# Two matrix layers behind a chunked attention: the second layer in two passes, each by Strassen's seven block products

## Chip, cores and metric

One core of one Trainium2 chip. The metric is the device time of one execution in microseconds (us); lower is better.

## What is computed

```python
def _moe_ref(x, w_in, w_out, alpha):          # first layer, 4608 tokens, 512 -> 2048 -> 512
    h = x @ w_in
    g = np.maximum(h, 0.0) + alpha * np.minimum(h, 0.0)
    return (g @ w_out).astype(np.float32)

def _moe2_ref(x, w_in, w_out):                # second layer, the same sizes
    h = x @ w_in
    g = np.where(h > 0.0, h, np.exp(np.minimum(h, 0.0)) - 1.0)
    return (g @ w_out).astype(np.float32)

def reference(...):
    attn_out = _attn_ref(q, k, v)             # softmax attention within chunks of 64 tokens, 8 batches x 8 heads
    x = attn_out.transpose(0, 2, 1, 3).reshape(B * S, H * D)
    return _moe2_ref(_moe_ref(x, ...), ...)
```

All weights come as float64 and are turned into float32 on the chip.

## The kernel before

Every large product is made of three matmuls: each operand is split into a high part that TensorE takes as it is (type fp32r) and a low part, the rest, and high x high, high x low and low x high are added up in PSUM. A split is one ScalarE copy (high) and one VectorE subtraction (low).

The 4608 tokens are nine blocks of 512 (`TB`), the 2048 inner features sixteen groups of 128 (`f`). One step of a block is `first(ph, j, f)` (L430: 4 input chunks x 3 matmuls of 128x512 into a bank `h`), the activation and split of its result (`after_first`), and `second(ph, j, f)` (L502: 4 output chunks x 3 matmuls into the four banks `acc`, which add up over the sixteen `f`). `ph` is the layer. Each matmul has its own load of a 128x128 operand.

The program is in three parts. `start()` puts out the beginning by a table of costs and due times (attention of the first tokens, the first layer's `first` of three blocks, the weights of layer one). `catch_up()` does the `second` of those blocks. `rest()` goes over the steps of both layers in a fixed order: at step s it issues `first` of step s + 2, one stage of the attention of the next block (`att_step`: scores, transposed weights by way of `turn` on VectorE and a pass through memory that `bring` fetches into `pbd`, product with v), and `second` of step s. `flush()` puts what engines other than TensorE do for a stage one stage later in the order. DMAs are all issued by SyncE's queue (SP), in order.

The second layer's weights are made during the first: at every second step `tick()` takes one 128x512 piece from float64 to float32 (two ScalarE operations, L150 and L175; three on VectorE, L157, L161 and L168; one on GpSimd, L180), and stores it (256 KB); `w_back` reloads the 32 pieces at the end of layer one and splits them into the tiles of layer one's weights, as these come free. The first layer's result goes to memory (`mid`), 512 tokens at a time, and is reloaded for the second layer. Both layers of a step stay on the chip: g is never stored in layer two.

Of the kernel before, what the change touches and what calls it, by code (L numbers as in the profile page):

```python
# [17 lines left out]
P = 128  # L18
CH = 64
SQ = 32  # L20
TB = 512

# [41 lines left out]
def tile_chunk_attention_prelu_elu(  # L64
# [27 lines left out]
    const = ctx.enter_context(tc.tile_pool(name="const", bufs=1))  # L92
    wp = ctx.enter_context(tc.tile_pool(name="wp", bufs=1))
    xp = ctx.enter_context(tc.tile_pool(name="xp", bufs=1))
    gp = ctx.enter_context(tc.tile_pool(name="gp", bufs=3))
    w64p = ctx.enter_context(tc.tile_pool(name="w64p", bufs=3))
    ldp = ctx.enter_context(tc.tile_pool(name="ldp", bufs=3))
    ap_ = ctx.enter_context(tc.tile_pool(name="ap", bufs=2))
    st_p = ctx.enter_context(tc.tile_pool(name="st", bufs=2))
    dram = ctx.enter_context(tc.tile_pool(name="dram", bufs=1, space=bass.MemoryType.DRAM))  # L100
    ps_acc = ctx.enter_context(tc.tile_pool(name="ps_acc", bufs=1, space=bass.MemoryType.PSUM))
    ps_h = ctx.enter_context(tc.tile_pool(name="ps_h", bufs=2, space=bass.MemoryType.PSUM))
    ps_a = ctx.enter_context(tc.tile_pool(name="ps_a", bufs=2, space=bass.MemoryType.PSUM))

    def w_tile(name, f, dtype=F32R):
# [6 lines left out]
    kbd = [const.tile([P, 2, NHP * 2, CH], F32, name="kbd0")]  # L112
    kbd += [w_tile("out", f, F32).rearrange("p c (h k) -> p c h k", k=CH) for f in (6, 7, 8)]
    pbd = const.tile([P, 2, NHP * 2, CH], F32, name="pbd")
    mid = [dram.tile([P, KDM, TB], F32, name=f"mid{j}") for j in range(NB)]
# [18 lines left out]
    pieces = [(1, "in", f, w1_in) for f in range(KFF)] + [(1, "out", f, w1_out) for f in range(KFF)]  # L134
    for f in range(KFF):
        pieces += [(2, "in", f, w2_in), (2, "out", f, w2_out)]
    raw, single = [], []

    def w_load():
        ph, name, f, w = pieces.pop(0)  # L140
        w64 = w64p.tile([P, KDM, P], I64, tag="w64", name="w64")
        nc.sync.dma_start(out=w64, in_=w_src(w, name, f))
        raw.append((ph, name, f, w64.rearrange("p k f -> p (k f)")))

    def w_abs():
# [20 lines left out]
    def w_join():  # L166
        words, t = single[-1][3:5]
        nc.vector.scalar_tensor_tensor(  # L168
            out=t, in0=words[:, 1], scalar=-0x40000000, in1=t, op0=ALU.bitwise_and, op1=ALU.bitwise_or
        )  # L170

    def w_low():

        words, low = single[-1][3], single[-1][5]
        nc.scalar.activation(out=words[:, 0], in_=low, func=AF.Copy, scale=2.0**-13)  # L175

    def w_add():

        words, t = single[-1][3:5]
        nc.gpsimd.tensor_tensor(out=t, in0=t, in1=words[:, 0], op=ALU.add)  # L180
# [8 lines left out]

    def tick():  # L190


        if single:
            ph, name, f, t = (single[0][i] for i in (0, 1, 2, 4))
            single.pop(0)
            nc.sync.dma_start(out=w_mid[name, f], in_=t.bitcast(F32))
        if len(raw) > 1 or raw and not pieces:
            w_abs()
            w_low()
            w_clamp()  # L200
            w_join()
            w_add()
        while pieces and len(raw) < 2:
            w_load()


    back, landed = [], []

    def w_back(most=3):
        while landed:  # L210
            name, f, t = landed.pop(0)
            wt[f"2{name}", f] = hl = w_hi(name, f, t)
# [13 lines left out]
    def load_qk(t):  # L226

        i = place(t)
        for c in range(2):
            nc.sync.dma_start(  # L230
                out=kbd[i][c * CH:(c + 1) * CH, c].rearrange("p h k -> p (h k)"),
                in_=kT[t, c * CH:(c + 1) * CH, :],
            )
        if i:
            qv = w_tile("out", 8 + i, F32)
            q_t[t], v_t[t] = qv[:, 0], qv[:, 1]
        else:
            q_t[t] = ldp.tile([P, NHP * 2 * CH], F32, tag="q", name="q", bufs=1)
        nc.sync.dma_start(out=q_t[t], in_=qT[t])

    def load_v(t):
        if not place(t):
            v_t[t] = ldp.tile([P, NHP * 2 * CH], F32, tag="v", name="v", bufs=1)
# [96 lines left out]
    def put_x(t, x):  # L340
        j, i = divmod(t, TPB)
        if i == 0:
            xf_t[1, j] = xp.tile([P, KDM, TB], F32, tag="xf", name="xf")
# [117 lines left out]
    def after_first(ph, j, f, h):  # L461
        if ph == 1:
            gf = prelu(f, h)
        else:
            gf = gp.tile([P, TB], F32, tag="gf", name="gf", bufs=2)

            nc.vector.tensor_scalar_min(gf, h, 0.0)  # L467
            nc.scalar.activation(out=gf, in_=gf, func=AF.Exp)  # L468
            nc.vector.scalar_tensor_tensor(  # L469
                out=gf, in0=gf, scalar=-1.0, in1=h, op0=ALU.add, op1=ALU.max  # L470
            )
# [16 lines left out]
    def second(ph, j, f):  # L488
# [6 lines left out]
        for e in range(KDM):  # L495
            a = slice(e * P, (e + 1) * P)
            if ph == 1:
                pairs = ((whi[:, a], ghi), (whi[:, a], glo), (wlo[:, a], ghi))
            else:
                pairs = ((ghi[:, a], whi), (ghi[:, a], wlo), (glo[:, a], whi))  # L500
# [6 lines left out]
        w_back(0)  # L507
        for e in range(KDM):
            if (ph, j) < (1, AHEAD) and e < 2:
                st = gp.tile([P, TB], F32, tag="gf", name="ost", bufs=2)  # L510
            elif (ph, j) < (1, AHEAD) or (ph, j) == (2, NB - 1) and e < 2:
                st = ldp.tile([P, TB], F32, tag="wt", name="ost", bufs=2)
            else:
                st = ldp.tile([P, TB], F32, tag="ld", name="ost")
            if (ph, j, e) == (2, NB - 1, KDM - 1):

                r0 = j * TB + e * P
                half = slice(0, TB // 2), slice(TB // 2, TB)
                nc.scalar.copy(st[:, half[0]], acc[e][:, half[0]])
                nc.vector.tensor_copy(st[:, half[1]], acc[e][:, half[1]])  # L520
                for queue, a in zip((nc.scalar, nc.sync), half):
                    queue.dma_start(out=out[r0:r0 + P, a], in_=st[:, a])
                return
# [4 lines left out]
            if ph == 1:  # L528
                nc.sync.dma_start(out=mid[j][:, e, :], in_=st)
            else:  # L530
                r0 = j * TB + e * P
                nc.sync.dma_start(out=out[r0:r0 + P, :], in_=st)

    def start():
# [38 lines left out]
        for i in range(2 * KFF):  # L573
# [168 lines left out]

    def rest():
        steps = [(ph, j, f) for ph in (1, 2) for j in range(AHEAD if ph == 1 else 0, NB) for f in range(KFF)]
        nxt = 2
        stages = []
        for s, (ph, j, f) in enumerate(steps):
# [14 lines left out]
            if (ph, j) == (1, NB - 1):  # L762
                back.append(("out", f))
            if ph == 1 and s % 2 == 0:
                tick()

            if (ph, j) != (1, NB - 1) or f not in range(KFF - 4, KFF - 1):
                w_back()
            b = 0 if (ph, j) == (1, NB - 1) else j + 1 if ph == 2 else NB
            if b < NB and f == 2:  # L770
                xf_t[2, b] = xp.tile([P, KDM, TB], F32, tag="xf", name="xf")
                nc.sync.dma_start(out=xf_t[2, b], in_=mid[b])

# [51 lines left out]
```

## Time and profile before

| | |
|---|---|
| median of 3 runs | 1679.34 us (1678.82 to 1680.45) |
| the profiled execution, span | 1679.1 us |
| TensorE matmuls (PE) | busy 1667.7 us, 99%, 8163 records |
| weight loads (PEld) | 1373.0 us, 82% |
| VectorE, ScalarE, GpSimd | 52%, 31%, 10% |
| DMA | 146 MB, mean 87 GB/s |

The busy time of an engine adds up the records of its instructions; a matmul's record lasts from its start to its modelled end and overlaps the next one's, and the loads of weights overlap the matmuls. The span runs from the first to the last instruction. PEclk is the granted clock of TensorE as a share of 2.4 GHz.

### The profile page before, as it was taken

What the parts mean: (1) busy time and instruction counts of PE and PEld (TensorE: products, weight loads), DVE (VectorE), ACT (ScalarE), POOL (GpSimd) and SP (SyncE); (2) the same over time, 40 slices, a digit from 0 to 9 for tenths busy, and PEclk for the clock granted to TensorE, in tenths of its full rate; (3) what the DMA queues carried; (4) which work ended last, traced back from release to release, by engine and by line L of the source; (5) the groups of instructions that cost most, each with busy time, mean ns of one, the idle gap of its engine ahead of it and who ended that gap; (6) DMA issues with size and microseconds to landing.
All of it is one profiled execution on the core that took longest, in us unless ns stands there. A gap on an engine that the chain in (4) does not pass through costs nothing.

```text
span 1679.1 us, 20843 instructions
## 1 busy us (share of the span) xinstructions
PE 1667.7 (99%) x8163; PEld 1373.0 (82%) x8163; DVE 868.2 (52%) x1374; ACT 522.9 (31%) x890; POOL 167.3 (10%) x144
## 2 busy tenths in 40 slices
PE   9999999999999999999999999999999999999999
PEld 7788887888888888888888888888888888888887
DVE  7868753456657566654444343434343434343443
ACT  5866422222223232311323232223222323222222
POOL 2322200011111111100242000000000000000000
PEclk9999999999999999999999999999999999999999
DMA  7756545344435443331332010101010101010000
GB/s 233 246 174 198 191 153 163 117 126 128 136 113 157 135 130 114 118 101 32 119 95 88 1 50 1 51 0 51 0 51 0 51 1 51 0 41 10 19 7 25
DMA packets 90002, 146.08 MB, mean 87 GB/s; under 512 B 9264, under 2 KB 38192, under 8 KB 88752
## 3 DMA queue, kind: packets, MB, share of 16 engines
q1 hardware_dynamic: 89760, 144.62, 27.1%
q8 instruction: 64, 1.05, 0.3%
q14 instruction: 34, 0.28, 0.1%
q10 hardware_dynamic: 144, 0.13, 0.0%
HBM read 98.57 MB, written 46.14 MB: 86 GB/s over the span
## 4 chain that ended last, share of the span: by engine, by line
PE 97%; ACT 1%; DVE 1%; DMA 1%; issue 0%; SPq 0%; POOL 0%; ACTq 0%; POOLq 0%; DVEq 0%
PE acc L502 46%; PE h L430 46%; PE x L332 2%; PE s L252 2%; PE unread L549 1%; ACT pbd L297 0%; DMA pbd<-p 0%; PE pt L291 0%; DMA p<-tp 0%; SPq L311 0%; ACT neg L445 0%; DVE mx L263 0%; DVE p L265 0%; DVE sm L274 0%; DVE sm L275 0%
## 5 line engine op out<-in xcount | busy, mean ns | idle before, releaser
L430 PE MATMUL h<-xhi,in 128*128 128x512 f32 x2176 | 713.6, 390 | 0.0
L430 PEld LDWEIGHTS h<-xhi,in 128*128 128x128 f32 x2176 | 408.6, 188 | 85.6 <-issue 0.9
L430 PE MATMUL h<-xlo,in 128*128 128x512 f32 x1088 | 424.1, 390 | 0.1
L502 PE MATMUL acc<-ghi,out 128*128 128x512 f32 x1152 | 375.6, 392 | 0.0
L502 PE MATMUL acc<-out,ghi 128*128 128x512 f32 x1152 | 354.9, 389 | 0.0
L477 ACT ACTIVATE ghi<-gf 128x512 fp32r<-128x512 f32 x240 | 151.6, 632 | 501.2 <-DVE gf L458 376.1
L482 DVE TENSOR_TENSOR glo<-gf,ghi 128x512 fp32r<-128x512 f32 x240 | 166.8, 695 | 182.7 <-ACT ghi L477 182.7
L502 PEld LDWEIGHTS acc<-ghi,out 128*128 128x128 f32 x1152 | 216.3, 188 | 48.6 <-issue 3.3
L502 PEld LDWEIGHTS acc<-out,ghi 128*128 128x128 f32 x1152 | 216.3, 188 | 44.8
L430 PEld LDWEIGHTS h<-xlo,in 128*128 128x128 f32 x1088 | 204.4, 188 | 43.0 <-DVE xlo L410 0.7
L468 ACT ACTIVATE gf<-gf 128x512 f32<-128x512 f32 x144 | 91.0, 632 | 448.5 <-DVE gf L467 448.5
L502 PE MATMUL acc<-glo,out 128*128 128x512 f32 x576 | 224.6, 390 | 0.0
L502 PE MATMUL acc<-out,glo 128*128 128x512 f32 x576 | 224.4, 390 | 0.0
L467 DVE TENSOR_SCALAR gf<-h 128x512 f32<-128x512 f32 x144 | 99.4, 690 | 220.3 <-PE h L430 220.3
L469 DVE SCALAR_TENSOR_TENSOR gf<-gf,h 128x512 f32<-128x512 f32 x144 | 99.1, 688 | 111.5 <-ACT gf L468 111.5
L455 DVE TENSOR_SCALAR gf<-h,alpha_sb 128x512 f32<-128x512 f32 x112 | 84.0, 750 | 138.7 <-PE h L430 138.2
L502 PEld LDWEIGHTS acc<-out,glo 128*128 128x128 f32 x576 | 108.2, 188 | 22.4
L502 PEld LDWEIGHTS acc<-glo,out 128*128 128x128 f32 x576 | 108.2, 188 | 21.5
L180 POOL TENSOR_TENSOR wt<-wt,w 128x512 int32<-128x512 int32 x64 | 84.7, 1323 | 386.6 <-DVE wt L168 203.3
L458 DVE SCALAR_TENSOR_TENSOR gf<-h,gf 128x512 f32<-128x512 f32 x112 | 77.4, 691 | 3.8
L280 POOL TENSOR_TENSOR p<-p,sm 128x512 f32<-128x512 f32 x32 | 36.2, 1130 | 264.8 <-DVE sm L276 259.2
L482 DVE TENSOR_TENSOR glo<-gl,ghi 128x512 fp32r<-128x512 f32 x48 | 32.8, 687 | 42.1 <-ACT ghi L477 42.1
(66 smaller groups left out, 950.1 us busy)
## 6 DMA issues: line engine op xcount, KB each, us to landing
w<-moe_w_in SPq DMA_DIRECT2D x32, 512.0 KB, 4.5
w<-moe_w_out SPq DMA_DIRECT2D x32, 512.0 KB, 4.1
gl<-g SPq DMA_DIRECT2D x48, 256.0 KB, 2.9
mid<-ost SPq DMA_DIRECT2D x36, 256.0 KB, 2.5
xf<-mid SPq DMA_DIRECT2D x9, 1024.0 KB, 5.2
out<-ost SPq DMA_DIRECT2D x35, 256.0 KB, 2.0
g<-pos SPq DMA_DIRECT2D x32, 256.0 KB, 2.8
kbd<-k_t SPq DMA_DIRECT2D x54, 128.0 KB, 2.8
```

The source lines that it names most:

```text
L180: nc.gpsimd.tensor_tensor(out=t, in0=t, in1=words[:, 0], op=ALU.add)
L252: nc.tensor.matmul(s[par * CH:(par + 1) * CH, hp], qq[:, h * CH:(h + 1) * CH], kbd[place(t)][:, :, h, :], start=True, stop=True,)
L280: (nc.vector if t < TPB else nc.gpsimd).tensor_tensor(out=p_t[t], in0=p_t[t], in1=sm, op=ALU.mult)
L430: nc.tensor.matmul(h, w[:, a], x, start=(kk == 0 and m == 0), stop=(kk == KDM - 1 and m == 2),)
L455: nc.vector.tensor_scalar(out=gf, in0=h, scalar1=0.0, scalar2=alpha_sb[:, f:f + 1], op0=ALU.min, op1=ALU.mult)
L458: nc.vector.scalar_tensor_tensor(out=gf, in0=h, scalar=0.0, in1=gf, op0=ALU.max, op1=ALU.add)
L467: nc.vector.tensor_scalar_min(gf, h, 0.0)
L468: nc.scalar.activation(out=gf, in_=gf, func=AF.Exp)
L469: nc.vector.scalar_tensor_tensor(out=gf, in0=gf, scalar=-1.0, in1=h, op0=ALU.add, op1=ALU.max)
L477: nc.scalar.activation(out=ghi, in_=gf, func=AF.Copy)
L482: nc.vector.tensor_sub(glo, gf, ghi.bitcast(F32))
L502: nc.tensor.matmul(acc[e], l, r, start=(f == 0 and m == 0), stop=(f == KFF - 1 and m == 2))
```

## The change

The first layer keeps its products. The second is done in two passes over all tokens: first all of x @ w_in with the activation, whose result g goes to memory (`gm`), then all of g @ w_out. Each pass takes 768 tokens at a time (six pairs of halves of 384, `HT`) and halves the summed dimension and the output dimension too, so that a product of 2x2 by 2x2 blocks comes from seven block products rather than eight (Strassen's scheme, in Winograd's form: four sums on either side, and sums of products, some of which PSUM does by adding a product onto an earlier one). In the first pass a step is one product of one quarter of 256 columns of each half: 12 matmuls of 128x384 (L945); in the second it is one product and one quarter of the summed dimension: 18 matmuls of 128x256 (L1044), with g as the loaded operand. Either has 28 steps for a token pair.

The seven combinations of the blocks of w_in and of w_out are made and split during the first layer, by the generator `convert` (80 pieces, of which `rest` takes one at each step but the last of a block), and stored split, 56 tiles of 512 KB (`w_mid`). They are brought back into the tiles of the weights that are done with (`bring_w2`). The sums of x and of g, their splits, the temporaries and the activation are done a step or more ahead or behind on VectorE and ScalarE. At the change of layer pools of tiles are closed and opened anew, the eight banks of PSUM with them: a0, a1, d and b of two banks each.

```diff
-    def tick():
...
-    def w_back(most=3):
...
+    def convert(cw, cb):
...
+            def split(k, src):
+                r = cb.tile([P, 2, KDM * P], F32R, tag="R", name="R")
+                nc.scalar.activation(out=shape(r[:, 0]), in_=src, func=AF.Copy)
+                nc.vector.tensor_sub(shape(r[:, 1]), src, shape(r[:, 0]).bitcast(F32))
+                m = u * NPROD + k if name == "in" else k * 4 + u
+                nc.sync.dma_start(out=w_mid[name, m], in_=r.bitcast(F32))
+
+            for t in (p0[:, 0], p0[:, 1], p1[:, 0]):
+                piece(t)
+                yield
+            piece(p1[:, 1])
+            split(0, a11)
+            yield
+            split(3, a12)
+            nc.vector.tensor_tensor(out=sm, in0=a21, in1=a22, op=ALU.add)
+            yield
...
     def rest():
-        steps = [(ph, j, f) for ph in (1, 2) for j in range(AHEAD if ph == 1 else 0, NB) for f in range(KFF)]
+        steps = [(1, j, f) for j in range(AHEAD, NB) for f in range(KFF)]
...
+        cw = open_pool("cw", conv, bufs=2, reuse_waits="tile")
+        cb = open_pool("cb", conv, bufs=1, reuse_waits="tile")
...
-            if ph == 1 and s % 2 == 0:
-                tick()
...
+            if f < KFF - 1:
+                next(ticks, None)
+            if j == NB - 1:
+                bring_w2("in", f)
+                if f >= 4:
+                    bring_w2("in", KFF + f - 4)
...
+                if 8 <= f < 13:
+                    prod(f - 8)
...
+    SUMS = {1: (X, Y, X), 2: (X, W, X), 4: (Y, W, Y), 5: (Z, Z, X)}
+    SRC = (X, X, X, Z, Y, W, Z)
...
+    def banks_for(k, a):
...
+        return bank["adabada"[k]]
...
+    def combine(k, acc, shape):
+        if k < 3:
+            temp[k] = slot(TEMP[k], f"t{k}", shape=shape)
+            nc.scalar.copy(temp[k], acc)
+        elif k < 6:
+            t = temp[k - 3]
+            nc.vector.tensor_tensor(out=t, in0=t, in1=acc, op=ALU.add)
+            return t
+        else:
+            return acc
...
+    def elu_exp(c):
...
+        nc.scalar.activation(out=r, in_=c, func=AF.Relu, scale=-1.0)
+        nc.scalar.activation(out=r, in_=r, func=AF.Exp, scale=-1.0)
+        return r
+
+    def elu_join(p, sw, k, c, r):
+        nc.vector.scalar_tensor_tensor(out=r, in0=r, scalar=-1.0, in1=c, op0=ALU.add, op1=ALU.max)
+        fh, th = QUARTER[k]
+        nc.sync.dma_start(out=gm[4 * fh + sw, 2 * p + th], in_=r)
+
+    def layer2_first():
...
+            for i in range(2):
+                for kk in range(2):
+                    a = slice((2 * i + kk) * P, (2 * i + kk + 1) * P)
+                    for m, (h, x) in enumerate(((0, xh), (0, xl), (1, xh))):
+                        nc.tensor.matmul(
+                            acc[:, i, :HT], w[:, h, a], x[:, kk, :],
...
+            c = combine(k, acc[:, :, :HT], (P, 2, HT))
...
+            if last:
+                if r >= 2:
+                    bring_w2("out", r - 2)
+                if 8 <= r < 12:
+                    g_bring(0, X, r - 8)
...
+    def layer2_second():
...
+            for i, t in order:
+                a = slice(t * P, (t + 1) * P)
+                whi, wlo = w[:, 0, i * HD:(i + 1) * HD], w[:, 1, i * HD:(i + 1) * HD]
+                for m, (l, x) in enumerate(((gh, whi), (gh, wlo), (gl, whi))):
+                    nc.tensor.matmul(
+                        acc[:, t * HD:(t + 1) * HD], l[:, i, a], x,
...
+            if prev:
+                finish(*prev)
+            prev = (p, k, acc) if q == 3 else None
+            g_sum(n + 3)
+            g_split(n + 2)
```

How the order of the instructions moves, at three places. The first is TensorE at the change of layer, in the changed kernel: the last four output chunks of layer one (L477), then the first step of the first pass (a is a pair of banks, w2in a split tile of combined weights).

```order
L477 MATMUL acc_7358<-ghi,out_2446 128x512
L477 MATMUL acc_7358<-glo,out_2446 128x512
L477 MATMUL acc_7358<-ghi,out_2446 128x512
L945 MATMUL a_7959<-xhi_7700,w2in_7383 128x384 [waits DMAHW5_49,DVE_49,Activation_49]
L945 MATMUL a_7959<-xlo_7701,w2in_7383 128x384
L945 MATMUL a_7959<-xhi_7700,w2in_7383 128x384 x2
L945 MATMUL a_7959<-xlo_7701,w2in_7383 128x384
```

The first product stands right behind the last matmul of layer one and waits for VectorE and ScalarE, which empty acc; before, the matmuls into `h` of the next block stood there.

The second is TensorE at the change of pass: the last matmuls of the first pass, then the second (w2out: combined weights, ghi and glo the loaded operand).

```order
L945 MATMUL a_10884<-xlo_10549,w2in_8046 128x384
L945 MATMUL a_10884<-xhi_10548,w2in_8046 128x384
L1044 MATMUL a_11040<-w2out_10531,ghi_10952 128x256 [waits DMAHW3_49,PE_49,Activation_49]
L1044 MATMUL a_11040<-w2out_10531,ghi_10952 128x256
L1044 MATMUL a_11040<-w2out_10531,glo_10953 128x256
```

The stream goes on into the other pair of banks, and waits for a weight tile and a split of g.

The third is VectorE in layer one, around the turn of the attention's weights (`STREAM_TRANSPOSE`). Before:

```order
L482 TENSOR_TENSOR glo<-gf,ghi 128x512 [waits Activation_49]
L157 TENSOR_SCALAR wt<-wt 128x512 [waits DMAHW4_49,Activation_49]
L161 TENSOR_SCALAR wt<-wt 128x512 [waits DVE_49]
L168 SCALAR_TENSOR_TENSOR wt<-w_3924,wt 128x512 [waits DMAHW2_49,DVE_49]
L455 TENSOR_SCALAR gf<-h,alpha_sb 128x512 [waits PE_49]
L458 SCALAR_TENSOR_TENSOR gf<-h,gf 128x512 [waits DVE_49]
L482 TENSOR_TENSOR glo<-gf,ghi 128x512 [waits Activation_49]
L303 STREAM_TRANSPOSE tp<-p 128x4x4x32 [waits DMAHW3_49,Pool_49]
L455 TENSOR_SCALAR gf<-h,alpha_sb 128x512 [waits PE_49]
```

In the changed kernel (P: a piece, S: a sum, R: the buffer of a split):

```order
L290 STREAM_TRANSPOSE tp<-p 128x4x4x32 [waits DMAHW6_49,Pool_49]
L161 TENSOR_SCALAR P_4990<-P_4990 128x512 [waits Activation_49]
L165 TENSOR_SCALAR P_4990<-P_4990 128x512 [waits DVE_49]
L171 SCALAR_TENSOR_TENSOR P_4990<-w_5114,P_4990 128x512 [waits DMAHW5_49,DVE_49]
L754 TENSOR_TENSOR R<-P_4989,R 128x512 [waits DMAHW0_49,Activation_49]
L442 TENSOR_SCALAR gf<-h,alpha_sb 128x512 [waits PE_49]
L445 SCALAR_TENSOR_TENSOR gf<-h,gf 128x512 [waits DVE_49]
L460 TENSOR_TENSOR glo<-gf,ghi 128x512 [waits Activation_49]
L754 TENSOR_TENSOR R<-P_4989,R 128x512 [waits DMAHW0_49,Activation_49]
L765 TENSOR_TENSOR S<-P_4990 128x512 [waits Pool_49]
L442 TENSOR_SCALAR gf<-h,alpha_sb 128x512 [waits PE_49]
```

Work on the weights stands behind every step's glo now, not every second one's, and a split waits for ScalarE and for a DMA.

## Rows read from the trace of the kernel before

**Rows 1.** The page: busy time by engine, and the chain that ended last, by engine.
```profile
PE 1667.7 (99%) x8163; PEld 1373.0 (82%) x8163; DVE 868.2 (52%) x1374; ACT 522.9 (31%) x890; POOL 167.3 (10%) x144
...
PE 97%; ACT 1%; DVE 1%; DMA 1%; issue 0%; SPq 0%; POOL 0%; ACTq 0%; POOLq 0%; DVEq 0%
```

**Rows 2.** Stretches: length, busy PE, PEld, DVE, ACT, POOL, granted clock, DMA share, GB/s.
```profile
0.00:35.00 35.00, 32.34 (x244) 24.37 (x245) 23.09 (x47) 17.13 (x28) 9.13 (x19) 1.00 0.77 237
340.00:860.00 520.00, 519.61 (x2733) 427.70 (x2732) 311.01 (x504) 138.26 (x239) 83.50 (x68) 1.00 0.38 116
892.00:1675.00 783.00, 783.00 (x3456) 648.65 (x3454) 328.89 (x483) 212.58 (x348) 10.23 (x8) 1.00 0.07 26
```

**Rows 3.** Costliest groups, layer two's matmuls and loads: operands, count | busy, mean ns.
```profile
L502 PE MATMUL acc<-out,ghi 128*128 128x512 f32 x1152 | 354.9, 389 | 0.0
...
L502 PEld LDWEIGHTS acc<-out,ghi 128*128 128x128 f32 x1152 | 216.3, 188 | 44.8
```

**Rows 4.** The chain in order of time, layers one and two: start, us, what.
```profile
165.05 2.72 PE acc L502 x12
...
1487.62 2.72 PE acc L502 x12
```

**Rows 5.** Timeline of PE, the first ten and the first nine matmuls: start, us, what.
```profile
1.45 4.63 PE L549 MATMUL unread<-zeros 128*128 128x512 f32 x10 [1.45 <-DVE zeros L544]
...
1.45 4.21 PE L549 MATMUL unread<-zeros 128*128 128x512 f32 x9 [1.45 <-DVE zeros L544]
```

**Rows 6.** Timeline of the weight loads, 29.5 to 31.2 us, after a pause.
```profile
30.13 0.19 PEld L430 LDWEIGHTS h<-xlo,in 128*128 128x128 f32 x1 [0.43 <-DVE xlo L615]
30.24 0.42 PEld L430 LDWEIGHTS h<-xhi,in 128*128 128x128 f32 x2
30.71 0.19 PEld L430 LDWEIGHTS h<-xlo,in 128*128 128x128 f32 x1
30.95 0.42 PEld L430 LDWEIGHTS h<-xhi,in 128*128 128x128 f32 x2
```

**Rows 7.** Timeline of the weight loads, 30 to 34 us: a stage of the attention.
```profile
32.89 0.85 PEld L252 LDWEIGHTS s<-out,out 128*64 128x64 f32 x16 [0.37 <-issue]
```

**Rows 8.** Groups of DVE and ACT by shape: busy, mean ns.
```profile
L527 DVE COPY ost<-acc 128x512 f32<-128x512 f32 x35 | 23.9, 685 | 35.8 <-DMA mid<-ost 11.9 <-PE acc L502 10.8 <-PE h L430 10.6
L520 DVE COPY ost<-acc 128x256 f32<-128x256 f32 x1 | 0.4, 424 | 1.1 <-ACT ost L519 1.1
L477 ACT ACTIVATE ghi<-gf 128x512 fp32r<-128x512 f32 x240 | 151.6, 632 | 501.2 <-DVE gf L458 376.1 <-DVE gf L469 116.7 <-PE acc L502 8.4
L525 ACT COPY ost<-acc 128x512 f32<-128x512 f32 x36 | 19.5, 581 | 14.6 <-PE acc L502 13.0 <-POOL out L188 1.7
L519 ACT COPY ost<-acc 128x256 f32<-128x256 f32 x1 | 0.4, 372 | 0.1
```

**Rows 9.** DMA: GB/s in 40 slices; issues, KB each, us to landing.
```profile
GB/s 233 246 174 198 191 153 163 117 126 128 136 113 157 135 130 114 118 101 32 119 95 88 1 50 1 51 0 51 0 51 0 51 1 51 0 41 10 19 7 25
...
w<-moe_w_out SPq DMA_DIRECT2D x32, 512.0 KB, 4.1
pbd<-p SPq DMA_DIRECT2D x96, 64.0 KB, 2.1
```

**Rows 10.** Timelines of DVE, SP and PE, 560 to 584 us: start, us, what.
```profile
566.59 0.42 DVE L157 TENSOR_SCALAR wt<-wt 128x512 f32<-128x512 f32 x1
...
569.16 0.75 DVE L455 TENSOR_SCALAR gf<-h,alpha_sb 128x512 f32<-128x512 f32 x1 [0.96 <-PE h L430]
572.03 0.70 DVE L303 STREAM_TRANSPOSE tp<-p 128x512 f32<-128x512 f32 x1
...
574.75 1.75 SPq L311 DMA_DIRECT2D pbd<-p  x4
...
579.93 1.09 PE L332 MATMUL x<-pbd,v 128*64 128x128 f32 x16
```

**Rows 11.** The chain's last pieces, in order of time.
```profile
1675.31 0.02 issue
```

More of the change, by code (lines that the diff above doesn't have):

```diff
@@ L21 @@
 TB = 512
+HT = 384
+NPROD = 7
+HD = 256
 COST = {
@@ L90, in tile_chunk_attention_prelu_elu, with open_pool @@
     scale = 1.0 / float(CH) ** 0.5
[L92 to L103, printed above, removed]
+    def open_pool(name, where=ctx, **kw):
+        return where.enter_context(tc.tile_pool(name=name, **kw))
+    const = open_pool("const", bufs=1)
+    wp = open_pool("wp", bufs=1)
+    dram = open_pool("dram", bufs=1, space=bass.MemoryType.DRAM)
+    early, conv, late, banks1 = (ctx.enter_context(ExitStack()) for _ in range(4))
+    attp = open_pool("attp", early, bufs=1)
+    ap_ = open_pool("ap", early, bufs=2)
+    w64p = open_pool("w64p", conv, bufs=3)
+    ldp = open_pool("ldp", conv, bufs=3)
+    xp = open_pool("xp", late, bufs=1, side="right")
+    gp = open_pool("gp", late, bufs=3, side="right")
+    st_p = open_pool("st", late, bufs=2, side="right")
+    ps_acc = open_pool("ps_acc", banks1, bufs=1, space=bass.MemoryType.PSUM)
+    ps_h = open_pool("ps_h", banks1, bufs=2, space=bass.MemoryType.PSUM)
+    ps_a = open_pool("ps_a", banks1, bufs=2, space=bass.MemoryType.PSUM)
     def w_tile(name, f, dtype=F32R):
@@ L120, in tile_chunk_attention_prelu_elu @@
     w_mid = {
-        (n, f): dram.tile([P, KDM * P], F32, name=f"w2{n}{f}") for n in ("in", "out") for f in range(KFF)
+        (n, m): dram.tile([P, 2, KDM * P], F32, name=f"w{n}_{m}") for n in ("in", "out") for m in range(4 * NPROD)
+    }
+    gm = {
+        (q, c): dram.tile([P, 2, HT], F32, name=f"gm{q}_{c}") for q in range(KFF // 2) for c in range(NT // HT)
     }
@@ L461, in after_first @@
     def after_first(ph, j, f, h):
[L462 to L471, printed above, removed]
+        gf = prelu(f, h)
         g_hi(ph, j, f, gf)
@@ L506, in second @@
             return
-        w_back(0)
         for e in range(KDM):
-            if (ph, j) < (1, AHEAD) and e < 2:
+            if j < AHEAD and e < 2 or j == NB - 1 and e < 2:
                 st = gp.tile([P, TB], F32, tag="gf", name="ost", bufs=2)
-            elif (ph, j) < (1, AHEAD) or (ph, j) == (2, NB - 1) and e < 2:
+            elif j < AHEAD:
                 st = ldp.tile([P, TB], F32, tag="wt", name="ost", bufs=2)
-            else:
[L514 to L523, printed above, removed]
+            elif j == NB - 1:
+                st = gp.tile([P, TB], F32, tag=("ghi", "glo")[e % 2], name="ost")
+            else:
+                if e % 2 == 0:
+                    pool, tag = conv_p[e // 2]
+                    both = pool.tile([P, 2, TB], F32, tag=tag, name="ost")
+                st = both[:, e % 2]
             if e % 2 == 0:
@@ new lines, in rest, with bring_w2 @@
+            if j == NB - 1:
+                bring_w2("in", f)
+                if f >= 4:
+                    bring_w2("in", KFF + f - 4)
+                if f == 6:
+                    assert next(ticks, 0) == 0
+                    open_early()
+                    x_load(0)
+                if 8 <= f < 13:
+                    prod(f - 8)
+        flush()
+    w2 = {}
+    sl = {}
+    pools2 = {}
+    W_SLOTS = [("in", f) for f in range(KFF)] + [("out", f) for f in range(KFF - 4)]
+    def bring_w2(name, m):
+        w2[name, m] = t = wp.tile([P, 2, KDM * P], F32R, tag="%s%d" % W_SLOTS[m], name=f"w2{name}{m}")
+        nc.sync.dma_start(out=t.bitcast(F32), in_=w_mid[name, m])
@@ new lines, in open_early, with open_late, slot @@
+    def open_early():
+        conv.close()
+        early.close()
+        pools2["E"] = open_pool("L2E", bufs=1, reuse_waits="tile")
+    def open_late():
+        late.close()
+        banks1.close()
+        pools2["L"] = open_pool("L2L", bufs=1, side="right", reuse_waits="tile")
+        pools2["ps"] = open_pool("ps2", bufs=1, space=bass.MemoryType.PSUM, reuse_waits="tile")
+    NE = 15
+    def slot(i, name, dtype=F32, shape=(P, 2, HT)):
+        if isinstance(i, tuple):
+            return wp.tile([P, 2, KDM * P], dtype, tag="%s%d" % i, name=name)[:, :, :HT]
+        return pools2["E" if i < NE else "L"].tile(list(shape), dtype, tag=f"s{i}", name=name)
@@ new lines, in take_sum, with prod_hi, prod_lo @@
+    def take_sum(tiles, k):
+        if k in SUMS:
+            o, a, b = (tiles(g) for g in SUMS[k])
+            nc.vector.tensor_sub(o, a, b)
+    def prod_hi(i):
+        p, k = divmod(i, NPROD)
+        hi, lo = PAIRS[i % len(PAIRS)]
+        xT[i] = hi, lo = slot(hi, "xhi2", F32R), slot(lo, "xlo2", F32R)
+        take_sum(lambda g: xq[p, g], k)
+        nc.scalar.activation(out=hi, in_=xq[p, SRC[k]], func=AF.Copy)
+    def prod_lo(i):
+        p, k = divmod(i, NPROD)
+        nc.vector.tensor_sub(xT[i][1], xq[p, SRC[k]], xT[i][0].bitcast(F32))
@@ new lines, in second_prep, with out_store @@
+    def second_prep(r):
+        if r == 24:
+            g_split(0)
+        if r == 26:
+            g_split(1)
+        if 24 <= r:
+            g_bring(0, Y, r - 24)
+    def out_store(p, k, t, parts=((0, 3, 0),)):
+        eh, th = QUARTER[k]
+        r0 = (2 * p + th) * HT
+        for a, b, queue in parts:
+            (nc.sync, nc.scalar)[queue].dma_start(
+                out=out[r0 + a * P:r0 + b * P, eh * HD:(eh + 1) * HD].rearrange("(t p) e -> p t e", p=P),
+                in_=t[:, a:b],
+            )
@@ new lines, in layer2_second @@
+    def layer2_second():
+        NTT = HT // P
+        total = NPAIR * NS2
+        prev = None
+        for q in range(4):
+            g_bring(0, W, q)
+        for n in range(total):
+            p, r = divmod(n, NS2)
+            k, q = divmod(r, 4)
+            end = n == total - 1
+            if q == 0:
+                acc = banks_for(k, p + NPAIR * 4).rearrange("p b c -> p (b c)")
+            gh, gl = gT.pop(n)
+            w = w2["out", r]
+            order = [(i, t) for t in range(NTT) for i in range(2)] if end else [(i, t) for i in range(2) for t in range(NTT)]
+            for i, t in order:
[4 more added lines that the diff above has]
+                        acc[:, t * HD:(t + 1) * HD], l[:, i, a], x,
+                        start=(k in STARTS and q == 0 and i == 0 and m == 0 and t % 2 == 0),
+                        stop=(q == 3 and i == 1 and m == 2), skip_group_check=True,
+                    )
+            if prev:
[3 more added lines that the diff above has]
+            g_split(n + 2)
+            if p + 1 < NPAIR:
+                for g, first in ((Y, 16), (X, 19), (W, 20), (Z, 24)):
+                    if first <= r < first + 4:
+                        g_bring(p + 1, g, r - first)
+            if n < 4:
+                g_bring(0, Z, n)
+            if n < 2:
+                bring_w2("out", NS2 - 2 + n)
+        p, k, acc = prev
+        t = slot(21, "last", shape=(P, NTT, HD))
+        view = acc[:, :NTT * HD].rearrange("p (t e) -> p t e", t=NTT)
+        for i in range(NTT):
+            if i % 2 == 0:
+                nc.scalar.copy(t[:, i], view[:, i])
+            else:
+                nc.vector.tensor_copy(t[:, i], view[:, i])
+            out_store(p, k, t, [(i, i + 1, 0)])
@@ L774, in tile_chunk_attention_prelu_elu, with finish @@
+    def finish(p, k, acc):
+        NTT = HT // P
+        c = combine(k, acc[:, :NTT * HD].rearrange("p (t e) -> p t e", t=NTT), (P, NTT, HD))
+        if k == 6:
+            t = slot(21, "last", shape=(P, NTT, HD))
+            nc.scalar.copy(t, c)
+            c = t
+        if k >= 3:
+            out_store(p, k, c)
     with tc.manual_schedule():
```

247 lines of the change are left out of this document (179 added, 68 removed).

## Prediction

> **What bounds the kernel now.** I read the page first: busy shares, then the chain that ended last. TensorE (PE) is busy for 99% of the span and makes up 97% of the chain [rows 1]; the reader is to see that no other engine has a share worth naming, so whatever PE's stream loses or gains is lost or gained by the kernel. Next comes the table by stretches: from 892 to 1675 us PE stands at 783.00 of 783.00 us with 3456 matmuls, which is exactly the second layer (9 token blocks x 16 steps x 24); in that stretch VectorE (DVE) is at 42%, ScalarE (ACT) at 27%, DMA at 0.07 [rows 2]. The costliest groups show those matmuls as 128x512 with a 128x128 load of weights each, of a record of 188 ns [rows 3]. The chain in order of time shows twelve in 2.72 us, in both layers [rows 4]. So one costs 783.0 / 3456 = 226.6 ns from start to start; its record of 389 ns overlaps the next.
>
> 512 columns at 2.4 GHz, the granted clock of 1.00 in [rows 2], are 213.3 ns; so 13.3 ns come on top. Of the first matmuls of the kernel the tenth adds 4.63 - 4.21 = 0.42 us, that is 512 columns at the lower level, 1.2 GHz (0.427), with nothing on top [rows 5]. What the 13.3 ns are, the trace doesn't say.
>
> **Layer two, the term that decides.** It loses 3456 matmuls of 512 columns (783.0 us). It gets 6 token pairs x 28 steps x 12 = 2016 matmuls of 384 columns, then 6 x 28 x 18 = 3024 of 256: 1,548,288 columns for 1,769,472 (seven eighths), but 5040 matmuls and loads of weights for 3456. No row shows a matmul of this kind with fewer than 512 columns, so I bound it:
> - 13.3 ns stay with each matmul: 160.0 + 13.3 = 173.3 and 106.7 + 13.3 = 120.0 ns; 2016 x 173.3 + 3024 x 120.0 = 349.4 + 362.9 = 712.3 us.
> - The excess goes with the columns (226.6 / 213.3 = 1.0625): 170.0 and 113.3 ns, 685.4 us. The lower bound.
> - The load of weights sets the pace: below, a rival.
>
> I take the first, as the nearer to a row: right after a pause the loads and streams are not yet in step and starts lie 0.23 to 0.24 us apart (30.71 to 30.95) with the same 512 columns [rows 6], so the excess belongs to how one matmul follows another rather than to the columns. Term: 712.3 - 783.0 = **-70.7 us**.
>
> Can a load keep up with 107 ns of columns? Where nothing holds it, the second load starts 0.11 us after the first (30.13, 30.24) though each record lasts 0.19 [rows 6]; so I take 110 ns as what it occupies, under 120. The attention's loads agree: sixteen of half the width fit into 0.85 us, 53 ns each [rows 7].
>
> The Trainium skill's "TensorE: Matmul & The Clock Gate", section Back-to-back issue gap, gives columns / 2.4 GHz + 2.5 ns for a warm matmul. By it 512 columns would take 215.8 ns and the new layer about 658 us (an estimate from that page); the row has 226.6, so the sum doesn't use it.
>
> **Layer one, where the new weights are made.** PE's work is the same. Eighty pieces of a generator now run, one in each step of two products (2 x 2.72 = 5.44 us [rows 4]), where before one in two steps had a tick. Removed: 32 stores of 256 KB and, late, 32 reloads with their splits. Added: 56 splits (ACT 0.63, DVE 0.69), 32 sums on DVE (0.69) and 56 stores of 512 KB. DVE: 88 x 0.69 = 61 us more in 340 to 860, 311 + 61 of 520 (72%); ACT 138 + 35 (33%); DMA 60 MB + 21 MB, some 157 GB/s where the page has 246 at most [rows 2, 8, 9]. So on average all is covered by PE. In detail: DVE waits 0.96 us for PE, up to 569.16, in a step whose tick began at 566.59 and so took 1.6 us [rows 10]; 2.5 us fit. A split with a sum is 1.4, a piece 1.6, the eight ticks with both 2.3.
>
> The tightest user is the attention: DVE turns p at 572.03, the turned tile is stored, pbd is brought from 574.75 to 576.50 and takes 2.1 us to land, 578.6; PE uses it at 579.93 [rows 9, 10]. That is 1.3 us of margin, and queued behind each split on DVE is this turn. All splits share one buffer R: ACT 0.63 + DVE 0.69 + the store. A 512 KB load takes 4.1 us to land [rows 9], so the ring is 5.4 us against a step of 5.44: just in time, and a split held up by R holds ACT's next ghi. On SP the store of R waits at the queue's head for DVE; the turn comes later on DVE anyway, so it adds nothing for pbd. I take **+3 us**; the bounds are 0 and 20 token tiles x 1.4 us = 28 us, if each turn comes one tick later with no margin left.
>
> **Seams.** Before, the evacuation of the last block's acc was hidden behind matmuls into other banks. Now the first product takes the banks of acc0 and acc1: the end of the last matmul plus 0.58 (ACT) and 0.69 (DVE) side by side [rows 8], **+1 us**. Between the two passes the stream goes on into the other bank pair. The tail after PE's end (1675.31 to 1679.1 [rows 11]) keeps its copy of 256 columns and its 128 KB store: 0.
>
> **Inside the passes.** Seven steps of the first pass last 7 x 12 x 173.3 = 14.6 us. ACT has 3 copies, 8 activations and 1.75 splits of 768 elements; with 372 ns at 256 and 581 at 512 a copy is 0.79 us, an activation 0.84: 10.6 us. DVE has 9.75 operations of 0.95 (424 and 685 ns at 256 and 512): 9.2 us [rows 8]. In the second pass 28 steps last 60.5 us, DVE has 47 x 0.95 = 44.5. Both stay hidden behind PE; the shortest wait, bank a from product 4 to product 6, has one step of 2.1 us for a DVE sum of 0.95. If a step's operations came late, that bank would stop PE. 0 us; bound 10.
>
> Sum: 1679.1 - 783.0 + 712.3 + 3 + 1 = **1612 us**. The profiled span of 1679.1 stands for a median of 1679.34, 0.2 us around it; I leave that out.
>
> **Rivals.**
> 1. *The load of weights becomes the bound* (slower). If a load occupies PE for its whole record of 188 ns [rows 3], 5040 x 188 = 947.5 us: 1679.1 - 783.0 + 947.5 + 4 = 1848 us. The point from which this side begins: 783.0 - 645.1 (the columns alone) over 5040 is 27.4 ns of excess per matmul, or, with 384 columns at 173.3, 143 ns for a matmul of 256. For it: PEld is busy 82% [rows 1], and each of the new matmuls has a shorter stream to hide it. Against: the starts 0.11 apart [rows 6], sixteen in 0.85 us [rows 7]. Chance 0.10. The Trainium skill's "Perfetto Trace Analysis", section Identifying the Most-Contended Engine, would have TensorE judged by the busy share of the weight loads rather than of the matmuls; by that rule this rival is the case, and the two rows above speak against it.
> 2. *The excess goes with the columns*: 1581 to 1585 us. For it: at the lower clock it is gone, as of a stream that is fed too slowly at the higher. Chance 0.10. With the page's gap for a matmul it would be some 1558 (an estimate from that page), 0.02 more.
> 3. *PE waits for what made no wait before*, still faster: layer one by up to 28 us (R and the turn, above); and the pair before the change of pass, where 26 weight tiles of 512 KB, 16 stores and 8 loads of 384 KB come to 23 MB in 58 us, 396 GB/s; the start of the kernel has 237 at a DMA share of 0.77 [rows 2], so 308 at most by that, and up to 17 us behind. Against: a weight tile is used 58 us after its place came free. 1617 to 1660 us. Chance 0.15.
> 4. *The change doesn't do what it says*: the order printed for PE shows 384 and 256 columns as counted, so what could be undone is the matmul's price alone (rival 1). 0.01, within 0.2%.
>
> **How the numbers follow.** Forecast 0.62, rivals 0.10 + 0.10 + 0.02 + 0.15 + 0.01. The range runs from the proportional bound, 1581, to 1650: the forecast with all 28 us of layer one and some ten of the passes. Left out: rival 1, the page's gap and the end of rival 3, some 0.15. A measurement of this kernel tells 0.2% from no change (3 us). Faster 0.89, within 0.2% 0.01, slower 0.10.
>
> **What would show it.** Twelve matmuls of 384 columns in 2.08 us and eighteen of 256 in 2.16; PE's waits in layer one under 5 us in all, most of them at x for pbd; DVE near 72% there; one wait of about 1 us at the first product; none at the change of pass. It is wrong if eighteen matmuls take over 2.6 us, or if PE waits for DVE, ACT or DMA by tens of us in either layer.

## The result, and the profile after

The changed kernel takes 1637.31 us (median of 4 runs, 1635.97 to 1638.0) where the kernel before takes 1679.08: a ratio of 0.9747, 95% interval 0.9733 to 0.9761. It is faster by 42 us, inside the range, with 67 forecast. The profiled span is 1634.2 us.

The page, busy time by engine, of the changed kernel:

```profile
PE 1618.7 (99%) x9747; PEld 1433.4 (88%) x9747; DVE 1067.6 (65%) x1493; ACT 730.5 (45%) x1070; POOL 129.3 (8%) x112
```

PE still bounds it [rows 1]. The stretches (columns as in [rows 2]): layer one, the first pass, the second pass.

```profile
340.00:860.00 520.00, 514.28 (x2633) 410.28 (x2632) 360.87 (x579) 156.43 (x272) 65.30 (x51) 0.99 0.44 147
...
920.00:1271.00 351.00, 351.00 (x2018) 350.09 (x2017) 206.52 (x227) 239.89 (x301) 0.00 (x0) 1.00 0.47 175
...
1271.10:1630.00 358.90, 358.75 (x3026) 358.22 (x3024) 256.72 (x283) 159.04 (x193) 0.00 (x0) 1.00 0.39 138
```

Layer two is what was hoped of it: 351.0 + 358.9 = 709.9 us for 783.0 [rows 2], with no idle time to speak of. But it begins at 920 us, not 892: layer one, whose products on PE the change leaves alone, takes 28 us longer. In 340 to 860 us PE gets through 2633 matmuls where it had 2733, and is idle for less than 6 us of the 520. The chain in order of time says why:

```profile
165.71 2.80 PE acc L477 x12
168.51 2.80 PE h L417 x12
...
1001.73 2.08 PE a L945 x12
...
1400.02 8.49 PE d L1044 x72
```

Twelve matmuls of layer one take 2.80 us instead of 2.72 [rows 4], from 165 us on, long before the first piece of a new weight is made (342.5 us): 233.3 ns each. Some 3070 of the 3456 ran so. From these rounded figures 3070 x 6.7 = 20.5 us, an estimate; the runs below put it at 18.4 to 18.9. What is left of the 28 begins in PE's list of waits:

```profile
PE h L417 <- DVE xlo L397: 5.7, 7, 1.9
PE x L319 <- ACT pbd L284: 3.0, 6, 1.3
PE unread L515 <- DVE zeros L510: 1.5, 1, 1.5
```

The second and third were there before, with the same 3.0 and 1.5 us. The first is new; VectorE's timeline around the first of these waits:

```profile
423.94 0.43 DVE L161 TENSOR_SCALAR P<-P 128x512 f32<-128x512 f32 x1 [1.26 <-ACT P L158]
424.40 0.43 DVE L165 TENSOR_SCALAR P<-P 128x512 int32<-128x512 int32 x1
424.87 0.69 DVE L171 SCALAR_TENSOR_TENSOR P<-w,P 128x512 int32<-128x512 int32 x1
425.48 0.68 DVE L754 TENSOR_TENSOR R<-P,R 128x512 fp32r<-128x512 f32 x1
426.08 0.68 DVE L261 TENSOR_REDUCE sm<-p 128x8 f32<-128x512 f32 x1
...
427.49 3.29 DVE L397 TENSOR_TENSOR xlo<-xf,xhi 128x512 fp32r<-128x512 f32 x4
```

PE's timeline of the same stretch:

```profile
425.92 0.40 PE L417 MATMUL h<-xhi,in 128*128 128x512 f32 x1
428.19 0.50 PE L417 MATMUL h<-xlo,in 128*128 128x512 f32 x1 [1.87 <-DVE xlo L397]
...
430.23 1.05 PE L417 MATMUL h<-xhi,in 128*128 128x512 f32 x2
```

A piece and a split for the new weights, with a wait for ScalarE, stand on VectorE between the scores and xlo at the end of a block; the next block's first product needs xlo at once. At two of the five block ends the granted clock then falls to its lower level for a while (columns as in [rows 2]):

```profile
428.00:432.00 4.00, 3.58 (x9) 2.37 (x10) 3.99 (x6) 0.63 (x1) 1.03 (x1) 0.59 0.06 26
631.00:633.00 2.00, 2.00 (x6) 1.52 (x6) 1.96 (x4) 0.00 (x0) 0.00 (x0) 0.50 0.00 0
```

### The profile page after: what moved, and what is told of

It reads as the page before. It is cut to its first block, busy times and chain, and to the rows that moved or that the text cites. A ratio compares the mean times of both kernels' runs of the same rounds, so it can differ in the third digit from the quotient of the medians.

```text
span 1634.2 us, 25035 instructions
## 1 busy us (share of the span) xinstructions
PE 1618.7 (99%) x9747; PEld 1433.4 (88%) x9747; DVE 1067.6 (65%) x1493; ACT 730.5 (45%) x1070; POOL 129.3 (8%) x112
## 4 chain that ended last, share of the span: by engine, by line
PE 94%; DVE 3%; ACT 1%; DMA 1%; issue 0%; SPq 0%; ACTq 0%; DVEq 0%
PE h L417 25%; PE acc L477 23%; PE a L945 12%; PE a L1044 12%; PE d L945 6%; PE d L1044 6%; PE b L1044 3%; PE b L945 3%; PE x L319 2%; PE s L239 2%; DMA g<-gm 1%; DVE xlo L397 1%; PE unread L515 1%; ACT pbd L284 0%; PE pt L278 0%
## 5 line engine op out<-in xcount | busy, mean ns | idle before, releaser
L477 PE MATMUL acc<-ghi,out 128*128 128x512 f32 x1152 | 382.1, 398 | 0.0
L417 PE MATMUL h<-xhi,in 128*128 128x512 f32 x1024 | 344.4, 399 | 0.0
L477 PEld LDWEIGHTS acc<-ghi,out 128*128 128x128 f32 x1152 | 216.4, 188 | 55.3 <-issue 3.4
L417 PEld LDWEIGHTS h<-xhi,in 128*128 128x128 f32 x1024 | 193.6, 189 | 47.2 <-issue 0.9
L477 PE MATMUL acc<-glo,out 128*128 128x512 f32 x576 | 227.8, 395 | 0.0
L1006 DVE TENSOR_TENSOR glo<-g,ghi 128x768 fp32r<-128x768 f32 x168 | 160.6, 956 | 87.4 <-ACT ghi L1005 86.5
L1005 ACT ACTIVATE ghi<-g 128x768 fp32r<-128x768 f32 x168 | 142.2, 847 | 164.2 <-PE a L1044 82.1
L417 PE MATMUL h<-xlo,in 128*128 128x512 f32 x512 | 204.7, 400 | 5.8 <-DVE xlo L397 5.7
L945 PE MATMUL a<-xhi,w2in 128*128 128x384 f32 x768 | 207.9, 336 | 0.0
L1044 PE MATMUL a<-w2out,ghi 128*128 128x256 f32 x1152 | 205.5, 281 | 0.0
L1044 PEld LDWEIGHTS a<-w2out,ghi 128*128 128x128 f32 x1152 | 176.7, 189 | 0.0
L1044 PE MATMUL a<-w2out,glo 128*128 128x256 f32 x576 | 161.7, 281 | 0.0
L945 PEld LDWEIGHTS a<-xhi,w2in 128*128 128x128 f32 x768 | 139.7, 188 | 0.9 <-ACT t L902 0.6
L477 PEld LDWEIGHTS acc<-glo,out 128*128 128x128 f32 x576 | 108.2, 188 | 25.1
L945 PE MATMUL a<-xlo,w2in 128*128 128x384 f32 x384 | 128.5, 335 | 0.0
L1044 PEld LDWEIGHTS a<-w2out,glo 128*128 128x128 f32 x576 | 108.8, 189 | 0.1
L945 PE MATMUL d<-xhi,w2in 128*128 128x384 f32 x384 | 105.3, 335 | 0.0
L1044 PE MATMUL d<-w2out,ghi 128*128 128x256 f32 x576 | 102.9, 281 | 0.0
```

The lines of the kernel that those rows point to most:

```text
L417: nc.tensor.matmul(h, w[:, a], x, start=(kk == 0 and m == 0), stop=(kk == KDM - 1 and m == 2),)
L477: nc.tensor.matmul(acc[e], l, r, start=(f == 0 and m == 0), stop=(f == KFF - 1 and m == 2))
L945: nc.tensor.matmul(acc[:, i, :HT], w[:, h, a], x[:, kk, :], start=(k in STARTS and kk == 0 and m == 0), stop=(kk == 1 and m == 2), skip_gr ...
L1005: nc.scalar.activation(out=hi, in_=src, func=AF.Copy)
L1006: nc.vector.tensor_sub(lo, src, hi.bitcast(F32))
L1044: nc.tensor.matmul(acc[:, t * HD:(t + 1) * HD], l[:, i, a], x, start=(k in STARTS and q == 0 and i == 0 and m == 0 and t % 2 == 0), stop=( ...
```

## The experiments

What could slow a matmul that is itself unchanged? The diff also rearranges the pools: `xp` and `gp`, which hold xhi, xlo, ghi and glo, the moving operands of layer one, go to the right end of SBUF. The program's own addresses: the weights begin on multiples of 256 bytes in both kernels; xhi and ghi did so before (156416 and 180992), and now begin 224 bytes past one (212960 and 196576). Against that stands the added traffic of VectorE, ScalarE and DMA as the cause.

**e1: the kernel before with the new places.**

```diff
-    xp = ctx.enter_context(tc.tile_pool(name="xp", bufs=1))
+    xp = ctx.enter_context(tc.tile_pool(name="xp", bufs=1, side="right"))
```
and the same for `gp` and `st`.

> The kernel before, with the tiles of x, of its splits and of g (xhi, xlo, ghi, glo) moved to the right end of SBUF as in the changed kernel, so that they begin 224 bytes past a multiple of 256 instead of on one; no instruction added or removed. Theory (the place of the moving operand sets the pace of the matmuls): twelve matmuls of 512 columns take 2.80 us instead of 2.72 in both layers, all but the 144 steps whose moving operand lies among the weights, so about 6700 x 6.6 ns = 44 us more, some 1723 us. Rival (the slower pace comes from the added traffic of the splits, sums and stores on VectorE, ScalarE and DMA): 1679 us, 2.72 us.

1722.74 us, ratio 1.0254 (1.0239 to 1.0269): 43 us slower. Its chain, in layers one and two:

```profile
171.45 2.80 PE acc L502 x12
...
1405.96 2.80 PE acc L502 x12
```

So the places alone are enough, with not one instruction more. Layer one's last matmul begins at 910.0 us here and at 891.6 in the kernel before: 18.4 us of the 43 are in that layer.

**e2 and e3: the changed kernel with its right-hand tiles shifted**, by 224 bytes (onto multiples of 256) and by 32 (onto multiples of 64).

```diff
+    edge = open_pool("edge", bufs=1, side="right")
+    edge.tile([P, 56], F32, name="edge")
     xp = open_pool("xp", late, bufs=1, side="right")
```

> The changed kernel with 224 bytes of padding at the right end of SBUF, so that the tiles there begin on a multiple of 256 bytes; nothing else. Theory (place): twelve matmuls of layer one go back from 2.80 to 2.72 us, 3070 x 6.7 ns = 20 us less; the passes of layer two change by less than 6 us either way; some 1617 us. Rival (traffic): 1637 us and 2.80 us.

> The same with 32 bytes of padding: the tiles at the right begin on a multiple of 64 bytes, but 192 past a multiple of 256. If 64 bytes are what counts: as with 224 bytes, some 1617 us and 2.72 us for twelve matmuls of layer one. If it must be a multiple of 256: 1637 us and 2.80 us.

e2: 1621.22 us, ratio 0.9652 (0.9636 to 0.9669), and layer one's twelve are back at

```profile
169.93 2.72 PE acc L479 x12
```

All the added traffic is still there, and the tiles still lie at the right end; so neither of them is what slowed the matmuls. Layer one's last matmul begins at 901.0 us, in the changed kernel at 919.8: the place is worth 18.9 us there.

e3, one run: 1637.66 us, and 2.80 as in the changed kernel. A multiple of 64 is not enough. e2 gains 16 us, not 20, partly because its second pass got slower,

```profile
1252.00:1615.00 363.00, 362.88 (x3023) 362.54 (x3021) 257.15 (x283) 158.56 (x192) 0.00 (x0) 1.00 0.38 136
```

363.0 / 3023 = 120.1 ns a matmul where the changed kernel has 358.9 / 3024 = 118.7. There the tiles of ghi and glo lie partly among the weights and partly at the right end, so that five ninths of the second pass's matmuls have their operands 224 bytes off. Aligned operands help 512 columns and hurt 256 a little.

**e4 and e7: the matmul by itself.** Two kernels of nothing but matmuls (the moving operand's tile is ma, mb, ...; the loaded one's la, lb, ...; each begins at its own offset), with one run of each kernel.

> No part of the computation: forty matmuls each, back to back, with 512, 384, 256, 192 and 128 columns, the moving and the loaded operand beginning 0, 32, 64, 96, 128 or 192 bytes past a multiple of 256. Theory (place): with 512 columns 226.7 ns where the moving operand begins on a multiple of 64 bytes, 233.3 where it begins 32 past one. For the width: if the excess of 13.3 ns stays with each matmul, 173.3 ns with 384 columns and 120 with 256; if it goes with the columns, 170.0 and 113.3; if the load of weights bounds the pace at its record, 188 ns with 256 and fewer. With 128 columns the load of 110 ns should bound in either case.

> No part of the computation: forty matmuls each again, the loaded operand always on a multiple of 256 bytes, the moving one 0 to 224 or 256 to 2048 bytes past one. Theory (only the difference of the two places modulo 256 counts): 226.7 ns with 512 columns at 0, 256, 512, 768, 1024 and 2048, more at all others; with 384 columns 173.3 at any; with 256 columns 120.0 at 0 and 1024 and 117 to 119 at others. Rival (some place takes the excess away): 216 ns at one of them.

PE's timeline of e4: start, us, forty matmuls each (eighty in the last row, 192 and 128 columns). The clock rises within the first row, which is left out here. Offsets: ma and la 0, mb and lb 32, mc and lc 64, md 96, me and le 128, mf 192.

```profile
16.60 9.50 PE L41 MATMUL acc<-mb,la 128*128 128x512 f32 x40
25.94 9.33 PE L41 MATMUL acc<-mc,la 128*128 128x512 f32 x40
35.10 9.49 PE L41 MATMUL acc<-md,la 128*128 128x512 f32 x40
44.44 9.49 PE L41 MATMUL acc<-me,la 128*128 128x512 f32 x40
53.77 9.48 PE L41 MATMUL acc<-mf,la 128*128 128x512 f32 x40
63.09 9.48 PE L41 MATMUL acc<-ma,lb 128*128 128x512 f32 x40
72.41 9.49 PE L41 MATMUL acc<-ma,lc 128*128 128x512 f32 x40
81.74 9.46 PE L41 MATMUL acc<-ma,le 128*128 128x512 f32 x40
91.04 9.28 PE L41 MATMUL acc<-mb,lb 128*128 128x512 f32 x40
100.15 7.10 PE L41 MATMUL acc<-ma,la 128*128 128x384 f32 x40
107.09 7.10 PE L41 MATMUL acc<-mb,la 128*128 128x384 f32 x40
114.02 7.11 PE L41 MATMUL acc<-ma,lb 128*128 128x384 f32 x40
...
127.93 4.95 PE L41 MATMUL acc<-ma,la 128*128 128x256 f32 x40
132.72 4.88 PE L41 MATMUL acc<-mb,la 128*128 128x256 f32 x40
137.44 4.89 PE L41 MATMUL acc<-ma,lb 128*128 128x256 f32 x40
...
146.95 9.04 PE L41 MATMUL acc<-ma,la 128*128 128x192 f32 x80
```

From one start to the next, over forty: 512 columns 233.5 ns with mb and la (25.94 - 16.60 = 9.34 us), as much the other way round (63.09 to 72.41), but with both at 32 9.11 us, 227.8 with the change from the case before in it. So it isn't either address that counts but their difference; both at 32 is the only such pair here. The expectation that a multiple of 64 is enough missed: 229.0 ns at 64 (25.94 to 35.10), but 233.3 at 128 and 233.0 at 192. With 64 on the loaded side it is 233.3, as at 192 on the moving one, which fits a difference taken modulo 256.

With 384 columns it is 6.94 / 40 = 173.5 ns aligned, 6.93 / 40 = 173.3 not. With 256 columns it is 4.79 / 40 = 119.8 ns aligned, 4.72 / 40 = 118.0 not; five ninths of 118.0 and four ninths of 119.8 make 118.8, close to the changed kernel's second pass. The eighty of 192 and of 128 columns take 9.04 us together and begin 111 ns apart at either width. A pace that doesn't go with the columns, and is near the 110 ns taken for a load, is that of the loads; they bound there, and not at 256 columns.

PE's timeline of e7, with la at 0 and the moving operand at 256 (ma), 512 (mb), 768 (mc), 16 (mg), 48 (mh), 4 (mk), 0 (ml), 96 (mm), 128 (mn) and 224 (mj):

```profile
34.55 9.23 PE L40 MATMUL acc<-ma,la 128*128 128x512 f32 x40
43.61 9.23 PE L40 MATMUL acc<-mb,la 128*128 128x512 f32 x40
52.68 9.23 PE L40 MATMUL acc<-mc,la 128*128 128x512 f32 x40
...
89.06 9.43 PE L40 MATMUL acc<-mg,la 128*128 128x512 f32 x40
98.32 9.36 PE L40 MATMUL acc<-mh,la 128*128 128x512 f32 x40
...
126.23 9.61 PE L40 MATMUL acc<-mk,la 128*128 128x512 f32 x40
135.68 4.96 PE L40 MATMUL acc<-ml,la 128*128 128x256 f32 x40
...
145.19 4.96 PE L40 MATMUL acc<-mm,la 128*128 128x256 f32 x40
149.99 4.91 PE L40 MATMUL acc<-mn,la 128*128 128x256 f32 x40
...
180.57 7.19 PE L40 MATMUL acc<-mn,la 128*128 128x384 f32 x40
187.60 7.11 PE L40 MATMUL acc<-mj,la 128*128 128x384 f32 x40
```

Every multiple of 256 gives 226.5 to 226.8 ns, 16 bytes 231.5, 4 bytes 236.3. No place came near 216 ns: the rival that some place takes the excess away fell for the places measured. Two expectations missed: 384 columns at a difference of 128 take 7.03 / 40 = 175.8 ns (180.57 to 187.60), not 173.3, and 256 columns at a difference of 96 take 4.80 / 40 = 120.0, as at 0, and not 117 to 119.

**e5 and e8: the block ends.** The piece at f = 13 moves to the last step of a block, in e2's kernel (e5) and in the unpadded one (e8).

```diff
-            if f < KFF - 1:
+            if f != KFF - 3:
                 next(ticks, None)
```

> The kernel of e2 (padding of 224 bytes) with the generator's piece at the last step of a block instead of at the step before the split of x (f = 13); the same 80 pieces. Theory (what remains of layer one's loss is the piece at f = 13, which puts up to 2.3 us of VectorE's work and its waits for ScalarE ahead of xlo, at five block ends): PE's waits for xlo fall from 6.3 us to under 1, no stretch at half clock follows them, layer one ends 7 to 9 us earlier, some 1613 us. Rival (the splits hold PE up all along layer one, by the turn of the attention or by R): less than 3 us.

> The changed kernel, without any padding, with only the piece at f = 13 moved to the last step of a block, as in e5. Theory (place and block ends are two causes that add up): PE's waits for xlo go, twelve matmuls of layer one still take 2.80 us; 5 to 8 us less than the changed kernel, some 1631 us. With PE slower by 2.9% the attention's operand should come in time here, without the waits for pbd that e5 and e6 have. Rival (the block ends cost time only where PE runs at its faster pace): 1637 us.

e8: 1629.28 us, ratio 0.9701 (0.9685 to 0.9717), 8 us under the changed kernel. e5: 1616.26 us, ratio 0.9622 (0.9608 to 0.9637), 5 us under e2, 3 short of what was expected. PE's waits for the attention after 330 us, in e8:

```profile
PE x L319 <- DMA pbd<-p: 1.9, 2, 1.2
```

All of PE's waits after 330 us in e5:

```profile
PE x L321 <- DMA pbd<-p: 4.4, 3, 1.7
PE h L419 <- DVE gf L447: 1.1, 2, 0.6
```

The waits for xlo are gone in both, and the mean granted clock of both is 1.000. So place and block ends are two causes that add up, but for what comes next: the attention's pbd is late three times. It takes both, PE at its faster pace and the piece at the last step: e2, with the piece where it was, waits 0.5 us for pbd, and e8, at the slower pace, 1.9. That e8 would not wait for it at all was wrong.

**e6: the best of both.** e5's kernel, with the padding in the stack of layer one's pools, so that layer two's tiles lie as in the changed kernel.

```diff
-    edge = open_pool("edge", bufs=1, side="right")
+    edge = open_pool("edge", late, bufs=1, side="right")
```

> The kernel of e5, but the padding goes away with layer one's tiles, so that the right-hand tiles of layer two begin 224 bytes past a multiple of 256 again, as in the changed kernel. Theory (at 256 columns a difference of place costs nothing and even gives a little): eighteen matmuls of 256 take 2.14 instead of 2.16 us, pass two 4 to 5 us less than in e5, pass one within 2 us; some 1608 us. Rival (aligned is always better): as e5 or slower.

1611.94 us, ratio 0.9600 (0.9584 to 0.9616): faster than both kernels and than every other one here, 25 us under the changed kernel. Its second pass takes 358.3 us where e5's takes 363.0, as expected; the total is 4 us over the expected 1608, about as much as e5's was over its own. Its waits for pbd (4.1 us in three) are left in; whether they can be had back isn't shown. With place and block ends set right the kernel comes to the forecast's 1612 us, with the few us of waits at pbd that the forecast had.

## Why the prediction was right, and where its size failed

- *The number.* The measured 1637 lies in the range because the range allowed for all 28 us of waits in layer one. It also lies in rival 3's interval of 1617 to 1660 us (chance 0.15); but of that rival's waits only some 9 us came. The larger part of the loss came from the pace of the matmuls, which no term and no rival names. That the 28 us are also the size of the loss is luck.
- *Layer two, -70.7 us.* Right: -73.1. The bound it chose, 13.3 ns on every matmul whatever its width, is what e7 and e4 show for operands that lie alike: 226.5, 173.5 and 119.8 ns. The proportional bound, 170.0 and 113.3, fell. The choice between the two was better than its reason: [rows 6] has 512 columns only and can't tell an excess per matmul from one per column; e4's 384 and 256 columns can. The difference of 2.4 us is 4.0 less in the second pass (118.7 ns, with five ninths at unequal places) and 1.6 more in the first.
- *The load of weights as the bound* (rival 1). It fell: a load occupies some 111 ns, by the 192 and 128 columns, 8 under what a matmul of 256 takes; the 110 ns taken from [rows 6] were right. PEld is at 358.2 of 358.9 us in the second pass, and yet the records overlap; neither that share nor the record of 188 ns said what it costs. The Trainium skill ("Perfetto Trace Analysis", Identifying the Most-Contended Engine) has TensorE judged by the busy share of the weight loads together with the share of peak arithmetic; the loads' share by itself, 99.8% in the second pass, would have misled here.
- *Layer one: "PE's work is the same".* This step failed. The instructions are the same, their pace isn't: 2.80 us for 2.72, since the pools' new sides set the moving operands 224 bytes off the loaded ones. That is 18.9 of the 28 us, by e2 (18.4 by e1). The prediction has no term for the diff's lines on the pools, and so puts what they move on PE at nothing, without a reason.
- *The waits in layer one, +3 us, named at pbd.* Some 9 us, at xlo: by that much layer one ends later in e2 than before (901.0 and 891.6 us). The ring on R and the margin at pbd, to which the working went, held in the changed kernel (R's store lands in 2.6 us, where 4.1 had been taken from a load); the split of x at a block's end, where xlo's four operations of VectorE (3.29 us) come just ahead of the matmuls that read them, has no term. What the piece and its split add there is some 2.2 us of VectorE and a wait for ScalarE; after two of the waits the lower clock added to it. When e5 took that away, pbd was next, as the margin of 1.3 us had it.
- *The seam, +1 us.* Nothing: the first product follows 0.23 us after the last matmul's start, so that its banks were free.
- *The passes, 0.* Right, but for about 1 us that PE lost in the first steps after the change of pass. Before that change DMA was full, as rival 3 had it. But it moved more than that rival's 308 GB/s: those came from the mean of a stretch, and were no ceiling, since slices of 0.9 us within the first 35 us of the kernel before reach 405. The changed kernel from 1240 to 1271 us (columns as in [rows 2]), and its GB/s in 40 slices of 1212 to 1271 us:

```profile
1240.00:1271.00 31.00, 31.00 (x181) 31.00 (x180) 15.67 (x18) 20.52 (x26) 0.00 (x0) 1.00 1.03 412
...
GB/s 267 227 160 244 259 331 289 11 0 0 280 333 356 415 346 365 407 405 420 418 352 358 434 409 419 417 419 419 418 417 421 419 419 417 421 403 418 422 419 410
```

Sum, against the rows of before: 1679.1 - 73.1 + 18.9 (place) + 9.4 (the rest of layer one) = 1634.3; measured 1634.2.

## What to carry to other kernels

Before work that "stays the same" is costed at its old pace, compare the addresses that the two programs give its operands: here lines that put pools on the other side cost about a quarter of what fewer products brought (18.9 of 73.1 us). With matmuls of 512 columns of fp32r, let moving and loaded operands lie a multiple of 256 bytes apart. Added work on a helper engine is to be placed by the tightest user of every stretch, block ends included; its mean load (72% forecast, 69% measured, 360.87 of 520) said nothing of it.

## What the runs showed of the hardware that was not expected

- The pace of back-to-back fp32r matmuls of 512 columns depends on the difference between the addresses of their two operands: 226.7 ns at multiples of 256 bytes, 229 to 237 at the others tried (4 to 224 bytes). At 384 columns the places tried gave 173.3 to 175.8 ns. At 256 columns equal places are among the slowest, by a little: 120 ns, and 117 to 120 at the others. Why is open.
- The excess over the columns is 13.3 ns at 512, 384 and 256 columns alike for equal places; with 192 and 128 columns a matmul takes 111 ns at either width, the loads' pace.
- DMA held 412 GB/s over 31 us (1240 to 1271 us of the changed kernel), in packets of 3.2 KB on average (12.77 MB in 3931). The 246 of [rows 9] is the most in slices of 42 us and says nothing of the peak: slices of 0.9 us of the kernel before reach 405.
